# Weight conversions given steps of their own, relu and square over two banks, and a new order of products in a float32 convolution and two-layer feed-forward kernel

## The chip, the cores and the metric

The kernel runs on 1 core of a Trainium2 chip. The metric is the device time of one execution in microseconds (us). The trace is one profiled execution; its times count from the start of the span.

## What is computed

A causal convolution over 7 positions, with softmaxed taps per head, is followed by two feed-forward layers. Both multiply tokens of width 192 by a 192 x 2048 matrix, apply a gate, and multiply by a 2048 x 192 matrix. Everything is float32 and there are 8192 tokens.

```python
out[b, s, c] = sum_k softmax(weight)[head(c), k] * x_pad[b, s + k, c]
# first layer (n = 1)
h = x @ w_in
g = np.where(h >= 1, h, np.where(h <= -1, 0.0, (h + 1) ** 2 / 4))
x = g @ w_out
# second layer (n = 2)
h = x @ w_in
g = h * (1.0 / (1.0 + np.exp(-1.702 * h)))
out = g @ w_out
```

## The kernel before

**Tiles.** The tokens are cut into 16 blocks of T = 512. The matrices are cut into NF = 16 tiles of 128 hidden channels, two of which form a *group* (NG = 8 groups a layer). The 192 channels are 128 (part a) and 64 (part b). A *phase* is one layer on one block, 32 in all, and a *unit* is one phase with one hidden tile, 512 in all. The list `units` (L252) holds their order. Two neighbouring units are a *step*: step s is units 2s and 2s + 1.

**Precision.** Each float32 operand is split into a high part and a low part (`split`, L74: ACT casts the high part, DVE subtracts to get the low part), and a product is made of hi x hi, lo x hi and hi x lo.

**A step on TensorE.** `both(u, v)` (L379) makes the hidden products of units u, u + 1 (into PSUM banks h) and the output products of units v = u - 4 and v + 1, two steps back (into the accumulators acc). Every matmul uses 64 of the 128 rows, so one on the lower rows (`low`) and one on the upper rows (`up`) run side by side; `couples` (L346) issues the two lists in turn, 19 pairs a step. Where a bank changes from one half of the rows to the other, a pause waits for an earlier matmul (`at_signal`). There are four h banks, so a bank is written again two steps later.

**The gate.** Behind the products of a step, `act_a` and `act_b` (L281, L295) are recorded for each of its two units: in the first layer a relu (L288) and a square (L289) on ACT and a max/min (L290) on DVE, in the second layer one gelu (L292) on ACT; then a cast to ghi on ACT (L75) and a subtraction to glo on DVE (L76). ghi and glo feed the output products two steps later.

**Weights.** The float64 words of a group are fetched by 7 DMAs on the SP queue (`weight_load`, L103) into one of three `raw` buffers, and turned into float32 by five operations (`weight_ops`, L121): scale on ACT (L134), shift and join on DVE (L137, L140), the cast of the high part (L146), and the subtraction of the low part on DVE (L151, L156). The cast runs on ACT, but on DVE for groups 2 to 7 of the first layer (`BY_DVE`). Groups 0 and 1 are converted in the prologue, in two column parts each.

**The order.** Everything is recorded in program order, and each engine works through its own list. `convert_at` (L541) gives a group a first and a last unit; `at` and `beside` (L554) put the operations behind the gate of that step. Groups 6 and 7 of the first layer have their cast and subtraction behind the gate of step 9 and of step 11; their first products are in step 10 and step 12.

**The prologue.** Block 0 is convolved by DVE, block 1 by products with diagonal matrices on all 128 rows (`conv_on_pe`, L188, bank ca_ps). `first_only` (L369) makes the hidden products of steps 0 and 1 without output products; in step 0 they stand between the tap products of block 1. `put_a(1, ca_ps)` splits that block into xah and xal, which step 2 needs.

Of the kernel before, what the change touches and what calls it, by code (L numbers as in the profile page):

```python
# [15 lines left out]
P = 128  # L16
# [4 lines left out]
def kernel(  # L21
# [32 lines left out]
    IN = DB + 3 * P  # L54
    BY_DVE = {(1, g) for g in range(2, NG)}

# [5 lines left out]
    xs_p = ctx.enter_context(tc.tile_pool(name="xs", bufs=4))  # L62
    a_p = ctx.enter_context(tc.tile_pool(name="a", bufs=3))
    g_p = ctx.enter_context(tc.tile_pool(name="g", bufs=LAG))
# [56 lines left out]
    def weight_ops(n, g, s, tiles, cols=whole):  # L121
        low, high = s[:, cols, 0], s[:, cols, 1]
        w = wt[n][:, g]
        hi = w[:, DB + cols.start : DB + cols.stop]
        main = slice(max(cols.start, DB), min(cols.stop, WC - DB))

        def a():
            return tiles()[0][:, cols]

        def d():  # L130
            return tiles()[1][:, cols]

        def scale():
            nc.scalar.activation(a(), f32(high), AF.Prelu, scale=2.0**-112, alpha=-(2.0**32))  # L134

        def shift():
            nc.vector.tensor_single_scalar(d(), low, 29, op=ALU.logical_shift_right)  # L137

        def join():
            nc.vector.scalar_tensor_tensor(  # L140
                d(), a().bitcast(U32), 3, d(), op0=ALU.logical_shift_left, op1=ALU.bitwise_or
            )

        def high_part():
            cast = nc.vector.tensor_copy if (n, g) in BY_DVE else nc.scalar.copy
            cast(hi, f32(d()))  # L146

        def low_part():
            made = f32(tiles()[1])
            lo, hi = (slice(k + main.start, k + main.stop) for k in (WC + DB, DB))  # L150
            nc.vector.tensor_sub(w[:, lo], made[:, main], f32(w[:, hi]))  # L151
            if cols.stop == WC:
                ends = made.rearrange("p (n c) -> p n c", c=DB)[:, :: WC // DB - 1]
                wb = w[:, 0 : WC + 2 * DB].rearrange("p (n c) -> p n c", c=DB)
                lo, hi = (wb[:, k : WC // DB + 2 - k : WC // DB + 1 - 2 * k] for k in (0, 1))
                nc.vector.tensor_sub(lo, ends, f32(hi))  # L156
# [94 lines left out]

    units = in_turn((0, 4), (1, 4), *((0, 2), (1, 2), (0, 2)) * 3, (1, 6))  # L252
    units += in_turn((2, 8), (3, 8), (2, 8), (3, 8))
# [26 lines left out]

    def act_a(u):  # L281

        n, _ = phases[units[u][0]]
        h = hid.pop(u)
        a = a_p.tile([P, T], F32, tag="a", name="a")
        if n == 1:

            nc.scalar.activation(a, h, AF.Relu, bias=0.5, scale=0.5)  # L288
            nc.scalar.activation(a, a, AF.Square)  # L289
            nc.vector.scalar_tensor_tensor(a, h, 1.0, a, op0=ALU.max, op1=ALU.min)  # L290
        else:
            nc.scalar.activation(a, h, AF.Gelu_apprx_sigmoid)  # L292
        act[u] = a

    def act_b(u):  # L295
        a = act.pop(u)
        hi = g_p.tile([P, T], F32R, tag="ghi", name="ghi")
        lo = g_p.tile([P, T], F32R, tag="glo", name="glo")
        split(a, hi, lo)
        halves[u] = (hi, lo)  # L300

# [30 lines left out]
    def gemm2_pieces(us):  # L332
# [4 lines left out]
        def pieces(rows):  # L337
            a, b = [], []
            for wh, wl, wb, hi, lo in parts:
                a += [(acc_a, wl[rows], hi[rows]), (acc_a, wh[rows], hi[rows]), (acc_a, wh[rows], lo[rows])]  # L340
                b += [(acc_b, wb[rows], hi[rows]), (acc_b, wb[rows], lo[rows])]
            return a + b

        return pieces(slice(0, H)), pieces(slice(H, P))

# [17 lines left out]
    def hidden_banks(u):  # L363
        banks = {}
        for w in (u, u + 1):
            hid[w] = banks[HID + w % 4] = bank(HID + w % 4, f"h{w}")
        return banks

# [10 lines left out]
    def both(u, v):  # L379
# [6 lines left out]
        (low0, up0, b0), (low1, up1, b1) = gemm1_pieces(u), gemm1_pieces(u + 1)  # L386
        low, up = gemm2_pieces((v, v + 1))
        low = low0 + b0 + low1 + low
        up = up + up0 + up1 + b1
        p, f = units[v]  # L390
# [4 lines left out]
        fresh = {HID + u % 4, HID + (u + 1) % 4, *(acc_banks(p) if f == 0 else ())}  # L395
        couples(low, up, banks, fresh, closing, {3, 12, 20, 30})

# [51 lines left out]

    def weights_at(n, g):  # L450
        ops = []

        def piece():
            if (n, g) in raw:
                made = []
                ops.extend(weight_ops(n, g, raw.pop((n, g)), lambda: made or made.extend(weight_tiles()) or made))
            ops.pop(0)()

        return [piece] * 5

# [14 lines left out]
    with tc.manual_schedule():  # L475
# [49 lines left out]
        straight, crossed, last, closing = first_only(0)  # L525
        run(a1[0], straight, a1[1], crossed, a1[2], lambda: last(closing), *a1[3:])
        run(*w0[1], lambda: put_b(1, cb_ps), *w1_[1][0:3])
        act_a(0)
        act_a(1)
        run(*w1_[1][3:])  # L530
        act_b(0)
        act_b(1)
        straight, crossed, last, closing = first_only(2)
        run(straight, last, lambda: crossed(closing))
        put_a(1, ca_ps)
        act_a(2)
        act_a(3)
        act_b(2)
        act_b(3)

        def convert_at(n, g, begin, end):  # L541
            at(begin - 8, lambda: fetch_w(n, g))
            scale, shift, join, high, low = weights_at(n, g)
            for unit, op in zip((begin, begin, begin + 1, end, end), (scale, shift, join, high, low)):
                at(unit, op)

        for g in range(2, NG):
            convert_at(1, g, 4 * g - 8, 4 * g - 6)
        for g, (begin, end) in enumerate(((24, 26), (28, 30), (32, 32), (34, 34), (38, 40), (42, 42), (44, 44), (46, 46))):
            convert_at(2, g, begin, end)  # L550
        for j in range(1, NBLK // B):
            conv_at(j)

# [10 lines left out]
        for u in range(LAG, len(units) + LAG + 4, 2):  # L564
            v = u - LAG
# [8 lines left out]
            beside(u // 2)  # L574
            finish_if_last(v + 1, u + 1)
# [55 lines left out]
```

## Time and profile before

| | |
|---|---|
| runs before, median (lowest to highest) | 1151.12 us (1151.05 to 1152.19), 3 runs |
| the profiled execution's own time | 1151.66 us |
| its span | 1149.9 us |
| instructions in the trace | 23746 |
| busy: TensorE matmuls (PE), weight loads (PEld) | 98%, 80% |
| busy: ScalarE (ACT), VectorE (DVE) | 72%, 62% |
| mean granted TensorE clock | 0.996 of full speed |

The span starts and ends with work of the engines; the profiled time has 1.76 us more around it. PE busy counts a pipelined matmul from its start to its modelled end, so two matmuls side by side, or one waiting behind another, both count as busy; what a step costs is read from the starts of its matmuls.

### The profile page before, as it was taken

Reading aid. Unit: us, or ns where it says so; the run is one execution under the profiler, and the core shown is the slowest. Engines: PE = TensorE matmul, PEld = TensorE weight load, DVE = VectorE, ACT = ScalarE, POOL = GpSimd, SP = SyncE. Lnnn points to the kernel's source line nnn. Section 1 sums busy time; section 2 is a strip of 40 time slices with the busy share of each in tenths; the row PEclk is TensorE's granted clock in tenths of the full one; section 3 lists DMA queues with packets and bytes.
Section 4 is the critical chain, followed back from the end, with each engine's and each line's share of the span. In section 5 each row is a group of like instructions: output and inputs, shape, how many; then the busy total and the mean of one; then the engine's idle time right before and its main releaser. Section 6 shows DMA issues by size and latency. Waiting matters only on the chain.

```text
span 1149.9 us, 23746 instructions
## 1 busy us (share of the span) xinstructions
PE 1130.4 (98%) x9738; PEld 919.7 (80%) x9738; DVE 713.2 (62%) x1100; ACT 825.9 (72%) x1437; POOL 5.9 (1%) x12
## 2 busy tenths in 40 slices
PE   9979999999999999999999999999999999999998
PEld 5756778888888888888888888888888888888886
DVE  7957677675655756567565765657566575655532
ACT  7848758885867768586775867767686775867754
POOL 2000000000000000000000000000000000000000
PEclk9989999999999999999999999999999999999999
DMA  5413302000010000100001000010001000000000
GB/s 158 128 56 87 98 1 75 2 10 20 15 47 15 2 22 14 47 15 10 24 11 38 15 20 15 14 43 6 20 15 47 15 1 19 15 19 15 11 15 15
DMA packets 26476, 34.90 MB, mean 30 GB/s; under 512 B 3840, under 2 KB 16384, under 8 KB 26368
## 3 DMA queue, kind: packets, MB, share of 16 engines
q1 hardware_dynamic: 26224, 33.26, 10.4%
q8 instruction: 77, 1.26, 0.5%
q14 instruction: 31, 0.25, 0.1%
q10 hardware_dynamic: 144, 0.13, 0.0%
HBM read 18.96 MB, written 6.29 MB: 22 GB/s over the span
## 4 chain that ended last, share of the span: by engine, by line
PE 92%; DVE 3%; ACT 3%; issue 1%; SPq 1%; DMA 1%; DVEq 0%; ACTq 0%
PE acc L355 47%; PE h L355 43%; SPq L114 1%; ACT a L288 1%; DVE a L290 1%; ACT a L289 1%; DMA raw<-in_w_dram 1%; DVE wt L151 1%; ACT ghi L75 1%; PE cb_ps L195 1%; PE ca_ps L195 0%; DVE glo L76 0%; PE acc L329 0%; DVE wd L140 0%; ACT wa L134 0%
## 5 line engine op out<-in xcount | busy, mean ns | idle before, releaser
L355 PE MATMUL acc<-ghi,wt 64*128 64x512 f32 x3048 | 928.5, 388 | 0.2 <-ACT ghi L75 0.2
L355 PE MATMUL acc<-glo,wt 64*128 64x512 f32 x2032 | 750.8, 387 | 0.9 <-DVE glo L76 0.9
L355 PE MATMUL h<-xah,wt 64*128 64x512 f32 x2048 | 631.1, 389 | 12.5 <-DVE wt L146 9.3
L355 PEld LDWEIGHTS acc<-ghi,wt 64*128 64x128 f32 x3048 | 520.6, 185 | 60.5 <-ACT ghi L75 1.0
L76 DVE TENSOR_TENSOR glo<-a,ghi 128x512 fp32r<-128x512 f32 x512 | 341.2, 688 | 223.0 <-ACT ghi L75 211.5
L355 PEld LDWEIGHTS h<-xah,wt 64*128 64x128 f32 x2048 | 376.1, 185 | 60.3 <-DVE wt L146 10.6
L355 PEld LDWEIGHTS acc<-glo,wt 64*128 64x128 f32 x2032 | 375.2, 185 | 42.3 <-DVE glo L76 2.5
L355 PE MATMUL h<-xal,wt 64*128 64x512 f32 x1024 | 395.1, 387 | 0.7 <-DVE xal L76 0.7
L75 ACT CAST ghi<-a 128x512 fp32r<-128x512 f32 x512 | 301.9, 615 | 33.5 <-DVE a L290 33.2
L355 PE MATMUL h<-xbh,wt 64*128 64x512 f32 x1024 | 313.9, 388 | 0.0
L290 DVE SCALAR_TENSOR_TENSOR a<-h,a 128x512 f32<-128x512 f32 x256 | 176.4, 691 | 174.1 <-ACT a L289 173.7
L292 ACT ACTIVATE a<-h 128x512 f32<-128x512 f32 x256 | 150.6, 596 | 140.3 <-PE h L355 121.7
L355 PEld LDWEIGHTS h<-xal,wt 64*128 64x128 f32 x1024 | 188.4, 185 | 21.2 <-DVE xal L76 1.1
L355 PEld LDWEIGHTS h<-xbh,wt 64*128 64x128 f32 x1024 | 188.0, 185 | 21.0 <-ACT wt L146 0.8
L355 PE MATMUL h<-xbl,wt 64*128 64x512 f32 x512 | 197.5, 387 | 0.0
L288 ACT ACTIVATE a<-h 128x512 f32<-128x512 f32 x256 | 152.3, 595 | 61.3 <-PE h L355 52.8
L289 ACT ACTIVATE a<-a 128x512 f32<-128x512 f32 x256 | 161.8, 632 | 8.2
L355 PEld LDWEIGHTS h<-xbl,wt 64*128 64x128 f32 x512 | 94.1, 185 | 10.4 <-DVE xbl L76 0.2
L177 DVE SCALAR_TENSOR_TENSOR cva<-xt,taps,cva 128x512 f32<-128x512 f32 x90 | 67.5, 750 | 1.7
L75 ACT CAST xbh<-s 64x512 fp32r<-64x512 f32 x16 | 9.9, 620 | 38.7 <-DVE s L407 38.7
L177 DVE SCALAR_TENSOR_TENSOR cvb<-xt,taps,cvb 128x512 f32<-128x512 f32 x42 | 31.4, 748 | 0.7
L75 ACT CAST xah<-cva 128x512 fp32r<-128x512 f32 x15 | 9.3, 620 | 11.3 <-DVE cva L177 11.3
(62 smaller groups left out, 240.2 us busy)
## 6 DMA issues: line engine op xcount, KB each, us to landing
raw<-in_w_dram SPq DMA_DIRECT2D x48, 128.0 KB, 2.4
xt<-in_xa_dram SPq DMA_DIRECT2D x16, 259.0 KB, 2.8
xbh<-xbh SPq DMA_DIRECT2D x31, 128.0 KB, 2.2
xbl<-xbl SPq DMA_DIRECT2D x31, 128.0 KB, 2.2
out_dram<-o SPq DMA_DIRECT2D x15, 256.0 KB, 2.0
raw<-in_w_dram SPq DMA_DIRECT2D x48, 64.0 KB, 2.3
raw<-in_w_dram SPq DMA_DIRECT2D x16, 192.0 KB, 2.7
out_dram<-o SPq DMA_DIRECT2D x17, 128.0 KB, 2.3
```

Of the source, the lines that this page charges most:

```text
L75: nc.scalar.copy(hi, src)
L76: nc.vector.tensor_sub(lo, src, f32(hi))
L114: nc.sync.dma_start(s[rows, at : at + count], w[rows, c : c + count])
L151: nc.vector.tensor_sub(w[:, lo], made[:, main], f32(w[:, hi]))
L177: return lambda: nc.vector.scalar_tensor_tensor(c, x, w, c, op0=ALU.mult, op1=ALU.add)
L195: return lambda: nc.tensor.matmul(c, d[k], t[:, k : k + T], start=fresh and k == 0, stop=k == n - 1)
L288: nc.scalar.activation(a, h, AF.Relu, bias=0.5, scale=0.5)
L289: nc.scalar.activation(a, a, AF.Square)
L290: nc.vector.scalar_tensor_tensor(a, h, 1.0, a, op0=ALU.max, op1=ALU.min)
L292: nc.scalar.activation(a, h, AF.Gelu_apprx_sigmoid)
L355: mm = nc.tensor.matmul(banks[n], w, r, start=n in fresh, stop=ends.get(n) == k)
```

## The change

The cast of the high part runs on ACT for all groups. `convert_at` takes a step for the fetch and one for each of the five operations; the ACT operations (scale, high) stand inside the gate of their step, between square and ghi, and the DVE operations (shift, join, low) before the gate of theirs. `gates` replaces `act_a` and `act_b`: relu and square are single instructions over the two banks of a step (128 x 1024). The two h banks of a step are one tile. The products of a step stand in another order, with three signals for four. The units of the first two phases come in another order, in which groups 6 and 7 are first used in steps 11 and 12. In the prologue the hidden products of step 0 stand together, the fetches of groups 2 and 3 are recorded before the rest of the prologue's conversions, and `put_a(1, ca_ps)` after the gate of step 0.

```diff
-    BY_DVE = {(1, g) for g in range(2, NG)}
-    a_p = ctx.enter_context(tc.tile_pool(name="a", bufs=3))
+    a_p = ctx.enter_context(tc.tile_pool(name="a", bufs=2))
+    def pair_of_banks(u):
+        k = u // 2 % 2
+        return ps.tile([P, 2, T], F32, tag=f"pair{k}", name=f"pair{k}")
         def high_part():
-            cast = nc.vector.tensor_copy if (n, g) in BY_DVE else nc.scalar.copy
-            cast(hi, f32(d()))
+            nc.scalar.copy(hi, f32(d()))
-    units = in_turn((0, 4), (1, 4), *((0, 2), (1, 2), (0, 2)) * 3, (1, 6))
+    units = in_turn((0, 4), (1, 4), *((0, 2), (1, 2)) * 2, (0, 4), (1, 2), (0, 4), (1, 6))
-    def act_a(u):
+    def gates(u, conversions=()):
...
+        a = a_p.tile([P, 2, T], F32, tag="a", name="a")
         if n == 1:
             nc.scalar.activation(a, h, AF.Relu, bias=0.5, scale=0.5)
             nc.scalar.activation(a, a, AF.Square)
-            nc.vector.scalar_tensor_tensor(a, h, 1.0, a, op0=ALU.max, op1=ALU.min)
+            for op in conversions:
+                op()
+            for k in (0, 1):
+                nc.vector.scalar_tensor_tensor(a[:, k], h[:, k], 1.0, a[:, k], op0=ALU.max, op1=ALU.min)
         else:
-            nc.scalar.activation(a, h, AF.Gelu_apprx_sigmoid)
+            for k in (0, 1):
+                nc.scalar.activation(a[:, k], h[:, k], AF.Gelu_apprx_sigmoid)
+            for op in conversions:
+                op()
+        for k in (0, 1):
...
+            split(a[:, k], hi, lo)
+            halves[u + k] = (hi, lo)
-        low = low0 + b0 + low1 + low
-        up = up + up0 + up1 + b1
+        low = low1 + low_b + low0 + b0 + low_a
+        up = up0 + up_a + up1 + b1 + up_b
-        couples(low, up, banks, fresh, closing, {3, 12, 20, 30})
+        couples(low, up, banks, fresh, closing, {6, 18, 37})
+    def convert_at(n, g, fetch, scale, shift, join, high, low):
...
+        for k, (where, step) in enumerate(((act, scale), (dve, shift), (dve, join), (act, high), (dve, low))):
+            where.setdefault(step, []).append(lambda k=k: piece(k))
+        for op in ((1, 2, 0, 0, 1, 1, 1, 2), (1, 3, 0, 2, 2, 3, 3, 4), (1, 4, 1, 4, 4, 5, 5, 6), (1, 5, 2, 4, 5, 6, 6, 7)):
+            convert_at(*op)
+        for op in ((1, 6, 4, 7, 7, 8, 8, 9), (1, 7, 5, 8, 8, 9, 9, 10), (2, 0, 7, 10, 11, 11, 11, 12)):
+            convert_at(*op)
+        for op in ((2, 1, 8, 11, 12, 13, 13, 14), (2, 2, 11, 13, 14, 15, 15, 16), (2, 3, 12, 15, 16, 16, 16, 17)):
+            convert_at(*op)
+        for g in range(4, NG):
+            k = 10 + 2 * g
+            convert_at(2, g, k - 3, k - 1, k, k, k, k + 1)
-        run(a1[0], straight, a1[1], crossed, a1[2], lambda: last(closing), *a1[3:])
+        run(*a1[0:4], straight, last, lambda: crossed(closing), *a1[4:])
+        run(*of(fetches, 0))
+        gates(0, [*w1_[1][4:], *of(act, 0)])
...
+        run(*of(fetches, 1), lambda: put_a(1, ca_ps), *of(dve, 1))
+        gates(2, of(act, 1))
...
                 both(u, v)
-                for op in (act_a, act_b):
-                    op(u)
-                    op(u + 1)
+                run(*of(fetches, step), *of(dve, step))
+                gates(u, of(act, step))
```

**VectorE around group 6 of the first layer.** Its words lie in raw_528 before and in raw_486 after the change, their integer halves in wd_790 and wd_692; h18 and h19 are step 9, h20 and h21 step 10. Before:

```order
L290 SCALAR_TENSOR_TENSOR a_846<-h18_802,a_846 128x512
L290 SCALAR_TENSOR_TENSOR a_850<-h19_803,a_850 128x512
L76 TENSOR_TENSOR glo_855<-a_846,ghi_854 128x512
L76 TENSOR_TENSOR glo_859<-a_850,ghi_858 128x512
L146 CAST wt1_88<-wd_790 128x768
L151 TENSOR_TENSOR wt1_88<-wd_790,wt1_88 128x640
L156 TENSOR_TENSOR wt1_88<-wd_790,wt1_88 128x2x64
L290 SCALAR_TENSOR_TENSOR a_907<-h20_865,a_907 128x512
```

The cast and the subtraction stood behind all of step 9's gate, and step 10's first product reads them. Now (a_761 is the gate of step 8, a_820 that of step 9; the group's first product is in step 11):

```order
L143 SCALAR_TENSOR_TENSOR wd_692<-wa_691,wd_692 128x768
L140 TENSOR_SCALAR wd_759<-raw_558 128x768
L294 SCALAR_TENSOR_TENSOR a_761<-pair0_708,a_761 128x512 x2
L79 TENSOR_TENSOR glo_769<-a_761,ghi_768 128x512
L79 TENSOR_TENSOR glo_773<-a_761,ghi_772 128x512
L153 TENSOR_TENSOR wt1_88<-wd_692,wt1_88 128x640
L158 TENSOR_TENSOR wt1_88<-wd_692,wt1_88 128x2x64
L143 SCALAR_TENSOR_TENSOR wd_759<-wa_758,wd_759 128x768
L294 SCALAR_TENSOR_TENSOR a_820<-pair1_776,a_820 128x512 x2
```

The cast has left VectorE, and the subtraction stands ahead of step 9's gate, two steps ahead of the first product.

**ScalarE around the gate of step 0** (raw_105 is group 1, raw_222 group 2, ca_ps block 1). Before:

```order
L134 ACTIVATE wa_162<-raw_105 128x320
L288 ACTIVATE a_237<-h0_196 128x512
L289 ACTIVATE a_237<-a_237 128x512
L288 ACTIVATE a_241<-h1_197 128x512
L289 ACTIVATE a_241<-a_241 128x512
L146 CAST wt1_88<-wd_163 128x320
L75 CAST ghi_248<-a_237 128x512
L75 CAST ghi_252<-a_241 128x512
L75 CAST xah_137<-ca_ps_116 128x512
```

Now:

```order
L137 ACTIVATE wa_162<-raw_105 128x320
L148 CAST wt1_88<-wd_163 128x320
L289 ACTIVATE a_252<-pair0_196 128x1024
L290 ACTIVATE a_252<-a_252 128x1024
L137 ACTIVATE wa_257<-raw_222 128x768
L78 CAST ghi_262<-a_252 128x512
L78 CAST ghi_266<-a_252 128x512
L78 CAST xah_137<-ca_ps_116 128x512
```

The cast of group 1 now precedes the relu, and a scale of group 2 stands between square and ghi; xah_137, which step 2's first product reads, is still behind both ghi.

## Rows read from the trace of the kernel before

**Rows 1.** The page's first part: busy us (share of the span) and instructions of TensorE.

```profile
PE 1130.4 (98%) x9738; PEld 919.7 (80%) x9738; DVE 713.2 (62%) x1100; ACT 825.9 (72%) x1437; POOL 5.9 (1%) x12
```

**Rows 2.** TensorE's timeline, first products of four steps: start us, us, engine, line, operation.

```profile
21.97 0.39 PE L355 MATMUL h<-xah,wt 64*128 64x512 f32 x1
...
598.14 0.39 PE L355 MATMUL h<-xah,wt 64*128 64x512 f32 x1
...
611.06 0.39 PE L355 MATMUL h<-xah,wt 64*128 64x512 f32 x1
```

**Rows 3.** Relus and gelus from 0 to 598.2 us: count, ns, first and last start.

```profile
L288 ACT ACTIVATE a<-h x144: 577/598/606, 16.8 to 589.9; 128x512 f32<-128x512 f32 x144
L292 ACT ACTIVATE a<-h x115: 575/598/609, 106.9 to 597.2; 128x512 f32<-128x512 f32 x115
```

**Rows 4.** TensorE's timeline, 60 to 88 us; idle before and what ended it in brackets.

```profile
60.15 0.39 PE L355 MATMUL h<-xbl,wt 64*128 64x512 f32 x1
...
64.46 0.50 PE L355 MATMUL h<-xah,wt 64*128 64x512 f32 x1 [3.93 <-DVE wt L146]
...
71.14 0.39 PE L355 MATMUL h<-xah,wt 64*128 64x512 f32 x1
...
79.73 0.79 PE L355 MATMUL h<-xah,wt 64*128 64x512 f32 x1 [4.11 <-DVE wt L146]
...
87.29 0.39 PE L355 MATMUL h<-xah,wt 64*128 64x512 f32 x1
```

**Rows 5.** A window: length, busy us (count) of PE, PEld, DVE, ACT, POOL, granted clock, DMA.

```profile
80.00:90.00 10.00, 10.00 (x62) 7.77 (x64) 2.62 (x5) 3.44 (x6) 0.00 (x0) 0.70 0.05 17
```

**Rows 6.** VectorE's timeline: the cast of group 6.

```profile
63.86 0.55 DVE L146 CAST wt<-wd 128x768 fp32r<-128x768 f32 x1
```

**Rows 7.** Waits: who for whom, us in total, times, longest.

```profile
PE h L355 <- DVE wt L146: 9.3, 3, 4.1
```

**Rows 8.** TensorE's timeline around step 16, the first of the second layer.

```profile
99.98 0.39 PE L355 MATMUL h<-xbl,wt 64*128 64x512 f32 x1
...
101.15 0.49 PE L355 MATMUL h<-xah,wt 64*128 64x512 f32 x1 [0.78 <-ACT xah L75]
...
106.44 0.39 PE L355 MATMUL h<-xbl,wt 64*128 64x512 f32 x1
```

**Rows 9.** Groups of instructions by form: busy us, mean ns, idle before and its releasers.

```profile
L75 ACT CAST ghi<-a 128x512 fp32r<-128x512 f32 x512 | 301.9, 615 | 33.5 <-DVE a L290 33.2
L290 DVE SCALAR_TENSOR_TENSOR a<-h,a 128x512 f32<-128x512 f32 x256 | 176.4, 691 | 174.1 <-ACT a L289 173.7
L289 ACT ACTIVATE a<-a 128x512 f32<-128x512 f32 x256 | 161.8, 632 | 8.2
L288 ACT ACTIVATE a<-h 128x512 f32<-128x512 f32 x256 | 152.3, 595 | 61.3 <-PE h L355 52.8
L134 ACT ACTIVATE wa<-raw 128x768 f32<-128x768 f32 x14 | 12.8, 912 | 0.0
L146 ACT CAST wt<-wd 128x768 fp32r<-128x768 f32 x8 | 6.7, 834 | 8.4 <-DVE wd L140 8.4
L146 ACT CAST wt<-wd 128x448 fp32r<-128x448 f32 x2 | 1.1, 565 | 0.6 <-DVE wd L140 0.5
```

**Rows 10.** ScalarE's timeline in the prologue.

```profile
19.08 0.44 ACT L146 CAST wt<-wd 128x320 fp32r<-128x320 f32 x1
19.43 1.14 ACT L75 CAST ghi<-a 128x512 fp32r<-128x512 f32 x2
```

**Rows 11.** VectorE's timeline in the prologue: the last join of group 1.

```profile
17.40 0.49 DVE L140 SCALAR_TENSOR_TENSOR wd<-wa,wd 128x320 uint32<-128x320 uint32 x1
```

**Rows 12.** The SP queue's timeline: nine fetches, and a copy of block 1.

```profile
5.39 4.58 SPq L114 DMA_DIRECT2D raw<-in_w_dram  x9
16.19 0.50 SPq L207 DMA_DIRECT2D xbh<-xbh  x1
```

**Rows 13.** The page's part on DMA issues: KB each, us to landing.

```profile
raw<-in_w_dram SPq DMA_DIRECT2D x48, 128.0 KB, 2.4
xbh<-xbh SPq DMA_DIRECT2D x31, 128.0 KB, 2.2
```

More of the change, by code (lines that the diff above doesn't have):

```diff
@@ L279, in gemm1_pieces @@
         return *a, [(h, hi_b[r], bh[r]), (h, lo_b[r], bh[r]), (h, hi_b[r], bl[r])]
-    def act_a(u):
+    def gates(u, conversions=()):
         n, _ = phases[units[u][0]]
         h = hid.pop(u)
-        a = a_p.tile([P, T], F32, tag="a", name="a")
+        a = a_p.tile([P, 2, T], F32, tag="a", name="a")
         if n == 1:
@@ L289, in act_a @@
             nc.scalar.activation(a, a, AF.Square)
-            nc.vector.scalar_tensor_tensor(a, h, 1.0, a, op0=ALU.max, op1=ALU.min)
-        else:
-            nc.scalar.activation(a, h, AF.Gelu_apprx_sigmoid)
[L293 to L300, printed above, removed]
+            for op in conversions:
+                op()
+            for k in (0, 1):
+                nc.vector.scalar_tensor_tensor(a[:, k], h[:, k], 1.0, a[:, k], op0=ALU.max, op1=ALU.min)
+        else:
+            for k in (0, 1):
[3 more added lines that the diff above has]
+        for k in (0, 1):
+            hi = g_p.tile([P, T], F32R, tag="ghi", name="ghi")
+            lo = g_p.tile([P, T], F32R, tag="glo", name="glo")
+            split(a[:, k], hi, lo)
+            halves[u + k] = (hi, lo)
     def acc_banks(p):
@@ L341, in pieces @@
                 b += [(acc_b, wb[rows], hi[rows]), (acc_b, wb[rows], lo[rows])]
-            return a + b
-        return pieces(slice(0, H)), pieces(slice(H, P))
+            return a, b
+        return *pieces(slice(0, H)), *pieces(slice(H, P))
     def couples(low, up, banks, fresh, closing, at_signal):
@@ L363, in hidden_banks @@
     def hidden_banks(u):
[L364 to L367, printed above, removed]
+        h = hid[u] = pair_of_banks(u)
+        return {HID + (u + k) % 4: h[:, k] for k in (0, 1)}
     def first_only(u):
@@ L386, in both @@
         (low0, up0, b0), (low1, up1, b1) = gemm1_pieces(u), gemm1_pieces(u + 1)
-        low, up = gemm2_pieces((v, v + 1))
-        low = low0 + b0 + low1 + low
-        up = up + up0 + up1 + b1
+        low_a, low_b, up_a, up_b = gemm2_pieces((v, v + 1))
+        low = low1 + low_b + low0 + b0 + low_a
+        up = up0 + up_a + up1 + b1 + up_b
         p, f = units[v]
@@ L439 @@
     plan, xt, raw = {}, {}, {}
+    dve, act, fetches = {}, {}, {}
     def at(unit, op):
@@ L448, in fetch_w, with piece @@
             weight_load(n, g, s, cols)
[L450 to L459, printed above, removed]
+    def convert_at(n, g, fetch, scale, shift, join, high, low):
+        ops, made = [], []
+        def piece(k):
+            if not ops:
+                tiles = lambda: made or made.extend(weight_tiles()) or made
+                ops.extend(weight_ops(n, g, raw.pop((n, g)), tiles))
+            ops[k]()
+        fetches.setdefault(fetch, []).append(lambda: fetch_w(n, g))
+        for k, (where, step) in enumerate(((act, scale), (dve, shift), (dve, join), (act, high), (dve, low))):
+            where.setdefault(step, []).append(lambda k=k: piece(k))
     def fetch_x(*which):
@@ L518, in b0_low, with of @@
             nc.scalar.copy(b0l[DB:P], f32(b0l[0:DB]))
+        for op in ((1, 2, 0, 0, 1, 1, 1, 2), (1, 3, 0, 2, 2, 3, 3, 4), (1, 4, 1, 4, 4, 5, 5, 6), (1, 5, 2, 4, 5, 6, 6, 7)):
[7 more added lines that the diff above has]
+            convert_at(2, g, k - 3, k - 1, k, k, k, k + 1)
+        for j in range(1, NBLK // B):
+            conv_at(j)
+        def of(ops, step):
+            return ops.get(step, [])
         w0, w1_ = parts_of(0), parts_of(1)
@@ L525 @@
         straight, crossed, last, closing = first_only(0)
-        run(a1[0], straight, a1[1], crossed, a1[2], lambda: last(closing), *a1[3:])
[L527 to L532, printed above, removed]
+        run(*a1[0:4], straight, last, lambda: crossed(closing), *a1[4:])
+        run(*of(fetches, 0))
+        run(*w0[1], lambda: put_b(1, cb_ps), *w1_[1][0:4])
+        gates(0, [*w1_[1][4:], *of(act, 0)])
         straight, crossed, last, closing = first_only(2)
         run(straight, last, lambda: crossed(closing))
[L535 to L552, printed above, removed]
+        run(*of(fetches, 1), lambda: put_a(1, ca_ps), *of(dve, 1))
+        gates(2, of(act, 1))
         def beside(step):
@@ L564 @@
         for u in range(LAG, len(units) + LAG + 4, 2):
-            v = u - LAG
+            v, step = u - LAG, u // 2
             if u < len(units):
                 both(u, v)
-                for op in (act_a, act_b):
-                    op(u)
-                    op(u + 1)
+                run(*of(fetches, step), *of(dve, step))
+                gates(u, of(act, step))
             elif v < len(units):
@@ L573 @@
                 gemm2(v + 1)
-            beside(u // 2)
+            beside(step)
             finish_if_last(v + 1, u + 1)
```

## The prediction

> **What bounds the kernel now.** I read the page first: TensorE's matmuls are busy 98% of the span [rows 1]. Busy counts overlapping matmuls, so I went to TensorE's own timeline and measured steps. In the middle of the run a step starts every 4.307 us: three steps lie between 598.14 and 611.06 [rows 2]. That is 0.227 us for each of its 19 pairs, evenly spaced, so nothing is lost there and the change removes no product. By 598.2 us, 259 relus and gelus have started, two a step [rows 3]; the last is the first of step 129, so the start at 598.14 is that of step 130. From step 2 at 21.97 [rows 2] that is 128 steps in 576.17 us. At 4.307 they would take 551.3. **24.9 us are lost, all in the early part; that is what there is to win.**
>
> The timeline of that part shows where. Step 9 ends at 60.15 + 0.23 = 60.38, but step 10 starts at 64.46, released by VectorE's cast of weights; step 13 starts at 87.29 [rows 4]. Steps 10, 11 and 12 thus take 26.91 us for 12.92: 14.0 lost. Two waits of 3.9 and 4.1 us are 8.0 of it; some 4 us more come from the clock, which the window behind the second wait shows at 0.70, a mixture of the 2.4 and 1.2 GHz levels [rows 5]; the rest is the subtraction behind the cast. The cast ran at 63.86 [rows 6], after step 10 should have begun, because it stood behind the whole gate of step 9, which needs step 9's products. Three waits on this cast make 9.3 us [rows 7]. Another place is step 16, the first of the second layer: its last pair starts 6.46 us after that of step 15 [rows 8], so 2.15 us are lost on the first layer's output being split. The other 8.8 us lie in smaller waits, mostly on weights and on ACT.
>
> **The change, part by part.**
>
> *Conversions in steps of their own.* Each group's last operation now stands ahead of a gate one to three steps before its first product, so by the order TensorE no longer meets it. This returns the 14.0 us of steps 10 to 12, clock included, and the waits on weights elsewhere. I count the whole 24.9 as returned, and now charge what comes in its place.
>
> *Step 2 starts later.* Step 2's first product needs xah of block 1, cast by ACT behind the gate of step 0. ACT's cast of group 1, which ran at 19.08 [rows 10], now precedes the relu and must wait for a join that ended at 17.40 + 0.49 = 17.89 [rows 11]. From there: cast 0.44, relu 1.03, square 1.06, scale 0.91, two ghi in 1.14 and xah 0.6 [rows 9, 10] end at 23.07, less up to 0.4 for overlap (two ghi take 1.14 where two durations are 1.23). That is 0.7 to 1.1 us later than 21.97, and xal behind it on DVE may add 0.3. I take **1.0**, bounds 0.7 to 1.4. Putting step 0's products together saves TensorE some switches between 128-row and 64-row work, but I cost it at nothing: step 2 waits for ACT all the same. On SP, 14 fetches of 4.58/9 = 0.51 us each [rows 12] now stand ahead of block 1's two copies. Only the second seven can be held, for group 0's buffer; if they began no earlier than the copy did before, at 16.19, the copies would go out at 19.8 and 20.3 and land 2.2 us later [rows 13], by 22.5. Their first use is pair 10 of step 2, after 25, so they stay hidden; a delay beyond 2.5 us would stall TensorE. POOL's list is not changed.
>
> *Relu and square over 1024 columns.* No row has this width. ACT's casts go from 565 ns at 448 columns to 834 at 768 [rows 9], 0.84 ns a column; 512 more columns make 595 into 1.03 us and 632 into 1.06. The lower bound is no growth (0.6), the upper one two whole instructions (1.19 and 1.26). By the slope, 128 first-layer steps save ACT 0.36 us each. In the steady state that is worth nothing, as TensorE is evenly fed already.
>
> *Does the gate still fit a step?* relu 1.03, square 1.06, a max/min on DVE 0.69, two ghi 1.24 [rows 9]: 4.02, with four handovers of some 0.04 about 4.2 us against 4.31. Now both h banks close at pair 14 of 19, where they closed at 12 and at 18. From that matmul's end, 3.6 us into the step, relu, square and two max/min end at 7.1, and the banks are due at 8.61: 1.5 us to spare. So plain steps cost **0**.
>
> *Gates with conversions.* In steps 2 to 15 ACT also runs nine scales (0.91) and eight casts (0.83); six casts have come from VectorE, where one took 0.55 [rows 6, 9]. One of them fits into ACT's wait for the max/min. Five steps (4, 8, 11, 13, 15) have two: 1.03 + 1.06 + 1.74 + 1.24 = 5.07, less five overlaps of 0.09, is 4.6 to 4.7, some 0.4 over a step. If the 1.5 us did not absorb any of it, five times 0.4 is **2.0**; bounds 0 and 3.
>
> *Step 16.* The same chain remains (copy, add, casts, a DMA of 2.2 us), behind a wider gate, and b1's products move from pairs 16 to 18 to pairs 12 to 14, 0.9 us sooner. The nearest row is its own loss of 2.15 [rows 8]; I take **2.3**, bounds 1.0 and 3.5.
>
> *Steps 17 to 28.* Second-layer weights now lead by at least one step. What stays is ACT and DVE sharing conversions with the next blocks' convolution: **1.0**, bounds 0 and 2.5.
>
> *The new order of products and signals.* The same 19 pairs. Every bank's change of halves still lies four pairs (0.9 us) behind the signalled matmul, and pauses at three pairs cost nothing before: **0**. A fetch lands 2.4 us after its issue [rows 13]; group 2's goes out right behind the prologue's fetches, and every later one stands two or three steps, 8.6 us or more, ahead of its scale: 0.
>
> *Sum.* 24.9 - 1.0 - 2.0 - 2.3 - 1.0 = 18.6 us. The profiled execution took 1151.66, which makes 1133.1; the median of the runs, 1151.12, lies 0.54 below it, so **1132.5**. With all low bounds 1.7 us are lost again (1127.9), with all high ones 10.4 (1136.6).
>
> **The rivals.**
>
> *ScalarE becomes the bound of steps 2 to 15.* Scale and cast stand between square and ghi, and ACT takes its list in order. If they fill no wait, a step costs 4.02 + (9 x 0.91 + 8 x 0.83)/14 = 5.1 us, 0.8 over, for 14 steps 11.4 instead of 2.0: 1141.9. For it: six casts are 0.28 us dearer here than on VectorE. Against it: the max/min takes 0.69, in which ACT is free, so one conversion a step costs nothing. Chance 0.11. The Trainium skill, "ScalarE: Activation LUTs", Rules for kernel authors, says the opposite of what the change does: cheap elementwise work such as relu, max and add belongs on VectorE. By that rule this rival would be the case; the rows support the price, 0.83 against 0.55 us for one cast, but not that VectorE had the room.
>
> *Slower: the wide instructions do not scale.* If a read over two banks costs well above two reads, the plain gate no longer fits. A step's 4.2 us may grow by 0.1. At 1.4 us each (0.36 above my price) the gate takes 4.9, 0.6 over; eight steps of a phase fall 4.8 behind, less 1.5 of slack 3.3, in 15 phases some 50 us: about 1182. It loses to before from about 1.25 us each. Against it: the slope over three widths, and two separate instructions would be 1.19 and 1.26 at most. Chance 0.04.
>
> *The waits on weights only move.* If a buffer or a late fetch makes one group late again, one such wait with its clock costs half of 14.0: 1139.5; both leave 1146.5. Against it: the fetch distances above. Chance 0.05.
>
> **How the numbers follow.** The forecast has 0.80. Its bounds reach from 1127.9 to 1136.6; going on towards the first and third rival to 1140 leaves out under 0.2: range 1128 to 1140. A measurement of this kernel can tell about 0.2%, 2.3 us. Faster by more: the forecast, the first rival and nearly all of the third, 0.93. Within 0.2%: 0.03, from mild cases of the second and bad ones of the third. Slower: 0.04.
>
> **What would show it.** Right: no matmul wait on weights above 1 us, a clock of 1.00 in all windows from 20 to 160 us, step 13 starting near 70 us, relu at 1.03 and square at 1.06, steps of 4.31 from 200 us on. Step 2 should start near 23, and step 16 should still show a wait on xah. The first rival would show steps of 5 us from 25 to 80 with PE waiting for ghi or h banks; the second, relu above 1.2 us and steps above 4.31 at 600 us. The forecast is wrong if the steady step changes at all, since some 240 of them follow the early part.

## The result and the profile after

The changed kernel takes 1133.56 us (median of five executions; 1133.43 to 1133.98), the kernel before 1151.69 us (median of six; 1151.05 to 1152.95). The ratio is 0.9842, 95% interval 0.9829 to 0.9856: 18.1 us, or 1.6%, faster. Forecast: 1132.5. (A sixth execution of the changed kernel took 2308.9 us, for a reason that no run here shows, and is left out.) The profile after is that of run 1 below, with a span of 1131.8 us.

TensorE has the same 9738 matmuls as in [rows 1] in a shorter span, and the relu and square are now 128 instructions each where [rows 9] had 256. From the page after:

```profile
PE 1122.0 (99%) x9738; PEld 934.4 (83%) x9738; DVE 698.0 (62%) x1094; ACT 781.8 (69%) x1187; POOL 5.9 (1%) x12
...
L289 ACT ACTIVATE a<-pair 128x1024 f32<-128x1024 f32 x128 | 131.2, 1025 | 32.4 <-PE pair L359 17.5
L290 ACT ACTIVATE a<-a 128x1024 f32<-128x1024 f32 x128 | 135.9, 1062 | 4.1
```

TensorE's timeline after shows where its time went. A step's first products are the `pair<-xah` row with x4. The rows are step 2, step 3, steps 12 and 13, steps 15, 16 (with a late pair inside it) and 17, steps 44 to 46, and step 130:

```profile
23.38 0.73 PE L359 MATMUL pair<-xah,wt 64*128 64x512 f32 x4 [1.01 <-ACT xah L78]
...
28.22 0.62 PE L359 MATMUL pair<-xah,wt 64*128 64x512 f32 x4
...
66.98 0.62 PE L359 MATMUL pair<-xah,wt 64*128 64x512 f32 x4
...
71.28 0.62 PE L359 MATMUL pair<-xah,wt 64*128 64x512 f32 x4
...
79.92 0.62 PE L359 MATMUL pair<-xah,wt 64*128 64x512 f32 x4
...
85.65 0.73 PE L359 MATMUL pair<-xah,wt 64*128 64x512 f32 x4 [1.24 <-ACT xah L78]
...
90.28 0.49 PE L359 MATMUL pair<-xbh,wt 64*128 64x512 f32 x1 [1.12 <-DMA xbh<-xbh]
...
91.76 0.84 PE L359 MATMUL pair<-xah,wt 64*128 64x512 f32 x4
...
208.44 0.64 PE L359 MATMUL pair<-xah,wt 64*128 64x512 f32 x4
...
214.09 0.73 PE L359 MATMUL pair<-xah,wt 64*128 64x512 f32 x4 [1.15 <-ACT ghi L78]
...
218.55 0.62 PE L359 MATMUL pair<-xah,wt 64*128 64x512 f32 x4
...
580.31 0.62 PE L359 MATMUL pair<-xah,wt 64*128 64x512 f32 x4
```

The four bracketed rows are all the waits that the view shows for TensorE from step 2 to 250 us. Both long waits of [rows 4] on a cast of weights are gone, and no wait on weights is left. From step 2 to step 130 it takes 580.31 - 23.38 = 556.93 us, against 551.3 for 128 steps at 4.307: **5.6 us lost where 24.9 were.** Step 2 starts 23.38 - 21.97 = 1.41 later, so 24.9 - 5.6 - 1.4 = 17.9 of the 18.1 us lie here. The window that stood at a granted clock of 0.70 [rows 5] now reads:

```profile
80.00:90.00 10.00, 7.91 (x65) 5.55 (x61) 9.01 (x15) 8.87 (x13) 0.00 (x0) 1.00 0.12 28
```

### The profile page after: what moved, and what is told of

It reads as the page before. It is cut to its first block, busy times and chain, and to the rows that moved or that the text cites. A ratio compares the mean times of both kernels' runs of the same rounds, so it can differ in the third digit from the quotient of the medians.

```text
span 2306.8 us, 23878 instructions
## 1 busy us (share of the span) xinstructions
PE 2301.7 (100%) x9738; PEld 1448.2 (63%) x9738; DVE 699.7 (30%) x1094; ACT 791.3 (34%) x1187; POOL 5.9 (0%) x12
## 4 chain that ended last, share of the span: by engine, by line
PE 100%; ACT 0%; DMA 0%; DVE 0%; issue 0%; ACTq 0%
PE acc L359 51%; PE pair L359 47%; PE cb_ps L197 1%; PE ca_ps L197 0%; PE acc L333 0%; DMA taps<-in_taps_dram 0%; ACT diag L194 0%; ACT o L436 0%; ACT taps L91 0%; DVE taps L95 0%; DVE taps L90 0%; DVE sm L93 0%; DVE mx L89 0%; DVE sm L92 0%; DVE sm L94 0%
## 5 line engine op out<-in xcount | busy, mean ns | idle before, releaser
L359 PE MATMUL acc<-ghi,wt 64*128 64x512 f32 x3048 | 1291.0, 671 | 0.0
L359 PE MATMUL acc<-glo,wt 64*128 64x512 f32 x2032 | 1038.8, 671 | 0.0
L359 PEld LDWEIGHTS acc<-ghi,wt 64*128 64x128 f32 x3048 | 749.7, 295 | 260.8 <-issue 235.7
L359 PE MATMUL pair<-xah,wt 64*128 64x512 f32 x2048 | 820.3, 671 | 0.2
L359 PEld LDWEIGHTS pair<-xah,wt 64*128 64x128 f32 x2048 | 452.7, 296 | 179.2 <-issue 134.7
L359 PE MATMUL pair<-xbh,wt 64*128 64x512 f32 x1024 | 529.0, 671 | 0.0
L359 PE MATMUL pair<-xal,wt 64*128 64x512 f32 x1024 | 514.5, 671 | 0.0
L359 PEld LDWEIGHTS pair<-xbh,wt 64*128 64x128 f32 x1024 | 301.0, 295 | 87.1 <-issue 80.6
L359 PE MATMUL pair<-xbl,wt 64*128 64x512 f32 x512 | 342.6, 672 | 0.0
L289 ACT ACTIVATE a<-pair 128x1024 f32<-128x1024 f32 x128 | 131.1, 1024 | 605.4 <-PE pair L359 585.0
L359 PEld LDWEIGHTS pair<-xal,wt 64*128 64x128 f32 x1024 | 226.6, 296 | 86.7 <-issue 80.4
```

What stands on the lines that cost most here:

```text
L359: mm = nc.tensor.matmul(banks[n], w, r, start=n in fresh, stop=ends.get(n) == k)
```

## Experiments

Each ran beside the kernel before on its chip; medians of it there were 1152.0 to 1152.3 us. The runs are on three chips, and a ratio's interval reaches some 1.7 us to either side, so a difference of 1 or 2 us between two of them is a hint and no more, unless their traces show where it comes from.

**1. The changed kernel once more.** No edit.

> The changed kernel once more, for its profile and time. The prediction: 1132.5 us; step 2 starts near 23, step 13 near 70 us, the granted clock stays at 1.00, step 16 waits for xah, and a step takes 4.31 us at 600 us. The rival of a bound ScalarE: 1142, with steps of about 5 us between 25 and 80 us.

Measured 1133.77 us, ratio 0.9842 (0.9825 to 0.9858). The rows above are from it, and the runs below are measured against it.

**2. Only the place of conversions, in the kernel before.** Everything else stays as before, the casts on DVE too.

```diff
-            convert_at(1, g, 4 * g - 8, 4 * g - 6)
+            convert_at(1, g, 4 * g - 10, 4 * g - 8)
```

> The kernel before, with one edit: the conversions of groups 2 to 7 of the first layer begin and end one step earlier, in the same engines and the same old order. If the 14.0 us of steps 10 to 12 came from the place of the conversions alone, waits and clock together, the two long waits shrink to under 2 us, the clock stays up, and the time falls by 9 to 13 us, to 1139 to 1143. If they came from ScalarE and VectorE being overloaded there, moving the work by a step only moves the waits, and the time stays within 3 us of 1151.

Measured 1140.36 us, ratio 0.9898 (0.9883 to 0.9913): 11.7 us from one step's shift. TensorE's waits on weights between 60 and 75 us shrink from 3.93 and 4.11 [rows 4] to these two, and the clock of that window is whole:

```profile
61.84 0.50 PE L355 MATMUL h<-xah,wt 64*128 64x512 f32 x1 [0.36 <-DVE wt L151]
...
71.07 0.50 PE L355 MATMUL h<-xah,wt 64*128 64x512 f32 x1 [0.28 <-DVE wt L151]
```

```profile
60.00:70.00 10.00, 9.64 (x83) 7.49 (x82) 8.86 (x15) 8.58 (x15) 0.00 (x0) 1.00 0.44 121
```

The shift has a price of its own, so 11.7 is what is left of more: the first product of step 4 now waits 1.30 us for a max/min on VectorE, and the clock falls in two windows, 30 to 40 and 90 to 100 us, that stood at 1.00 in the kernel before.

```profile
32.70 0.50 PE L355 MATMUL h<-xah,wt 64*128 64x512 f32 x1 [1.30 <-DVE a L290]
```

```profile
30.00:40.00 10.00, 8.55 (x59) 6.34 (x57) 9.58 (x17) 8.47 (x16) 0.00 (x0) 0.83 0.67 194
...
90.00:100.00 10.00, 9.42 (x68) 8.18 (x70) 7.21 (x12) 7.72 (x13) 0.00 (x0) 0.83 0.40 106
```

So the place of first-layer conversions makes two thirds of the gain, without the wide instructions, the new order of products or the casts on ACT. How the other third is shared out is only in part known: the new place of the second layer's conversions was not tried by itself.

**3. The reverse: only two subtractions put back, in the changed kernel.** The last subtractions of groups 6 and 7 go behind the gate of the step before their use; `tail` is a new table whose operations run behind `gates`.

```diff
-        ... ((act, scale), (dve, shift), (dve, join), (act, high), (dve, low))
+        ... ((act, scale), (dve, shift), (dve, join), (act, high), (tail if n == 1 and g > 5 else dve, low))
-        (1, 6, 4, 7, 7, 8, 8, 9), (1, 7, 5, 8, 8, 9, 9, 10)
+        (1, 6, 4, 7, 7, 8, 8, 10), (1, 7, 5, 8, 8, 9, 9, 11)
                 gates(u, of(act, step))
+                run(*of(tail, step))
```

> The changed kernel with only two operations moved: the last subtractions (VectorE, some 0.9 us each) of first-layer groups 6 and 7 stand behind the gate of the step before their first product (steps 10 and 11, products at steps 11 and 12), the place that conversions had in the kernel before. By my theory a gate's last subtraction ends some 4 us into the next step, so TensorE waits about 4 to 5 us at step 11 and as long at step 12, two waits as in the kernel before, and the granted clock falls behind them, which costs some 4 us more: 1145 to 1149. Rival A (the clock does not follow from such waits): the waits alone, 1142 to 1144, with a clock of 1.00 in 60 to 90 us. Rival B (an operation's place counts little, the number of operations on VectorE and ScalarE beside the gates is what matters): within 2 us of 1133.7.

Measured 1147.73 us, ratio 0.9960 (0.9946 to 0.9973): 14.0 us slower than the changed kernel. TensorE's timeline shows steps 11 (from 62.61), 12 (from 73.19) and 13, and the windows of it the granted clock, the column behind the engines:

```profile
62.61 0.39 PE L359 MATMUL pair<-xah,wt 64*128 64x512 f32 x2
67.62 0.80 PE L359 MATMUL pair<-xah,wt 64*128 64x512 f32 x2 [4.62 <-DVE wt L153]
...
73.19 0.39 PE L359 MATMUL pair<-xah,wt 64*128 64x512 f32 x2
78.75 0.79 PE L359 MATMUL pair<-xah,wt 64*128 64x512 f32 x2 [5.16 <-DVE wt L153]
...
85.51 0.62 PE L359 MATMUL pair<-xah,wt 64*128 64x512 f32 x4
```

```profile
67.00:70.00 3.00, 2.38 (x12) 1.91 (x14) 2.19 (x4) 0.00 (x0) 0.00 (x0) 0.52 0.20 52
70.00:73.00 3.00, 3.00 (x28) 2.45 (x26) 0.00 (x0) 0.51 (x1) 0.00 (x0) 0.91 0.62 168
...
81.00:84.00 3.00, 3.00 (x16) 2.30 (x14) 0.00 (x0) 0.00 (x0) 0.00 (x0) 0.50 0.03 5
84.00:87.00 3.00, 3.00 (x28) 2.50 (x26) 0.06 (x1) 2.09 (x2) 0.00 (x0) 0.96 0.00 0
```

Two steps take 85.51 - 62.61 = 22.90 us for 8.61, so 14.3 are lost, nearly what steps 10 to 12 lost before (14.0). The waits are 4.62 + 5.16 = 9.8 of it. Of the other 4.5 us, 4.2 come behind the waits: 18 pairs stand between 67.62 and 73.19, and 18 between 78.75 and 85.51, which take 5.57 and 6.76 us where 18 at 0.227 take 4.08. There the clock reads 0.50 to 0.52 at first, the 1.2 GHz level, and 16 matmuls start in 3 us where 28 do at 0.96. Both rivals fall: the clock follows these waits (A), and no operation was added (B). The Trainium skill, "TensorE: Matmul & The Clock Gate" (HAM oscillation — how this bites in real kernels), describes such a chain, with waits for DMA: TensorE waits for data, and the work behind the wait starts at half clock. The rows at 0.50 agree.

**4. Relu and square as one instruction per bank**, the rest as changed.

```diff
-            nc.scalar.activation(a, h, AF.Relu, bias=0.5, scale=0.5)
-            nc.scalar.activation(a, a, AF.Square)
+            for k in (0, 1):
+                nc.scalar.activation(a[:, k], h[:, k], AF.Relu, bias=0.5, scale=0.5)
+                nc.scalar.activation(a[:, k], a[:, k], AF.Square)
```

> The changed kernel, with relu and square again as one instruction for each bank (four of 512 columns for two of 1024). The prediction's reason (the wide form saves ScalarE 0.36 us a step, but TensorE is not waiting for it): at most 2 us slower than the changed kernel, no more than a few waits of under 0.5 us between 55 and 100 us. The rival (ScalarE is the bound of steps 2 to 15, and the wide form is what makes the gates fit): 14 steps of 0.36, 5 us slower or more.

Measured 1134.8 us (1134.03 to 1135.41), ratio 0.9851 (0.9837 to 0.9866): 1.0 us slower by the medians, while its profiled execution has the span of run 1's (1131.9 against 1131.8). The wide instructions as such are worth little, if anything.

**5. The old order of products and signals**, the rest as changed.

```diff
-        low = low1 + low_b + low0 + b0 + low_a
-        up = up0 + up_a + up1 + b1 + up_b
+        low = low0 + b0 + low1 + low_a + low_b
+        up = up_a + up_b + up0 + up1 + b1
-        couples(low, up, banks, fresh, closing, {6, 18, 37})
+        couples(low, up, banks, fresh, closing, {3, 12, 20, 30})
```

> The changed kernel, with the products of a step in the order of the kernel before and its four signals. The prediction costed the new order at nothing in itself; but with gates over both banks the old order closes the second bank at pair 18 instead of 14, so relu starts 0.9 us later, and the first output products are due at pair 0 instead of 3. By the spare time of 1.5 us a plain step still fits and the steady step stays at 4.31 us; waits of up to 0.5 us appear in steps with conversions and splits, 1 to 12 us in all. If the order of products mattered to the pace of the pairs itself, the steady step would change at 600 us: by 0.05 us for 240 steps, 12 us, either way.

Measured 1146.92 us, ratio 0.9958 (0.9943 to 0.9973): 13.1 us slower, a little past the range I had given. The plain step is 4.31 us long, and yet every first-layer phase lost time. ScalarE's timeline of one phase, and the wait it causes on TensorE:

```profile
548.88 1.03 ACT L289 ACTIVATE a<-pair 128x1024 f32<-128x1024 f32 x1 [2.19 <-PE pair L359]
...
553.19 1.03 ACT L289 ACTIVATE a<-pair 128x1024 f32<-128x1024 f32 x1 [0.21 <-PE pair L359]
...
557.31 0.59 ACT L426 COPY o<-acc 64x512 f32<-64x512 f32 x1
557.92 0.59 ACT L429 COPY o<-acc 128x512 f32<-128x512 f32 x1
558.40 1.03 ACT L289 ACTIVATE a<-pair 128x1024 f32<-128x1024 f32 x1
...
584.13 1.09 ACT L297 ACTIVATE a<-pair 128x512 f32<-128x512 f32 x2 [0.21 <-PE pair L359]
```

```profile
562.00 0.47 PE L359 MATMUL pair<-xah,wt 64*128 64x512 f32 x1 [0.23 <-ACT ghi L78]
```

Relus start 4.31 apart, until two copies of the finished phase's output stand in front of one: it starts 5.21 behind its predecessor. The eight steps take 584.13 - 548.88 = 35.25 us; in the changed kernel and in second-layer phases they take 34.45. So 0.8 is lost once in each of the 12 first-layer phases behind 236 us, some 9 us; the rest is lost before that. The same two copies stand in front of a relu in the changed kernel too. There it starts 5.27 behind its predecessor, and the phase still takes 34.46 us (first relu 540.87, first gelu of the next phase 575.33):

```profile
545.15 1.03 ACT L289 ACTIVATE a<-pair 128x1024 f32<-128x1024 f32 x1
...
550.42 1.03 ACT L289 ACTIVATE a<-pair 128x1024 f32<-128x1024 f32 x1
```

In the old order the second bank closes with pair 18, in the new one both are closed by pair 14; those four pairs, 0.9 us, are room that the copies need. The old order also has its first output products, which read ghi, at pair 0 instead of 3, so ghi is due 0.7 us sooner; no run changes that alone.

**6. The old order and, besides, one instruction per bank** (the edits of 5 and 4 together).

> The changed kernel with the old order of products and signals (as the run that took 1146.9) and, besides, relu and square as one instruction per bank, so that the first relu can start when the first h bank closes, at pair 12, and not with the second at pair 18. If the 13 us that the old order costs come from the wide relu having to wait for both banks: a first-layer phase is back at 34.45 us for 8 steps and the time is 1134 to 1140. If they come from the order itself (the banks' changes of halves, the signals, the late close of the second bank): a phase stays near 35.2 and the time at 1145 to 1148.

Measured 1138.79 us, ratio 0.9888 (0.9871 to 0.9904). A first-layer phase takes 34.55 us, so 8.1 of the 13.1 us return, though the output products still come at pair 0. Most of the cost thus comes from a wide relu that has to wait for the later of two banks. With 4 and 5 this gives a table (us):

| | wide relu and square | one per bank |
|---|---|---|
| new order | 1133.8 | 1134.8 |
| old order | 1146.9 | 1138.8 |

The new order is worth 4.0 us with separate instructions and 13.1 with wide ones; the wide ones lose 8.1 in the old order, and what they gain in the new one, 1.0, is too little to tell. Neither price exists by itself.

**7. The six casts back on VectorE**, at the same place in the list.

```diff
-            nc.scalar.copy(hi, f32(d()))
+            (nc.vector.tensor_copy if (n, g) in {(1, k) for k in range(2, NG)} else nc.scalar.copy)(hi, f32(d()))
```

> The changed kernel, with the six casts of first-layer groups 2 to 7 given back to VectorE (0.55 us each there, 0.83 on ScalarE), in the same place: between the gate's squares and its max/min. My theory: in the changed kernel ScalarE is 9.0 to 9.8 us busy in each 10 us from 20 to 80 us, and yet steps 3 to 15 take 4.31, so relieving it gains nothing; on VectorE the casts stand ahead of the gate's max/min, which frees the h banks. Time 1133 to 1136. Rival (ScalarE as the bound, by which such work belongs on VectorE): it gains some of the 3 us that the early part still loses, 1130 to 1132.5.

Measured 1134.75 us (1134.62 to 1134.92), ratio 0.9848 (0.9834 to 0.9863): 1.0 us slower by the medians, and certainly no gain. ScalarE is freer, but VectorE is at 9.70 of 10 us where it was at 9.10, and new waits on ghi appear at steps 8 and 11 (the window is 50 to 60 us, columns as in [rows 5]):

```profile
50.00:60.00 10.00, 10.00 (x90) 8.49 (x90) 9.70 (x17) 9.49 (x13) 0.00 (x0) 1.00 0.37 102
```

```profile
49.76 0.73 PE L359 MATMUL pair<-xah,wt 64*128 64x512 f32 x4 [0.25 <-ACT ghi L78]
...
63.29 0.72 PE L359 MATMUL pair<-xah,wt 64*128 64x512 f32 x4 [0.30 <-ACT ghi L78]
```

**8. The old order of units** in the first two phases.

```diff
-    units = in_turn((0, 4), (1, 4), *((0, 2), (1, 2)) * 2, (0, 4), (1, 2), (0, 4), (1, 6))
+    units = in_turn((0, 4), (1, 4), *((0, 2), (1, 2), (0, 2)) * 3, (1, 6))
```

> The changed kernel with the old order of units in steps 4 to 15 (groups 4 and 6 of block 0's first layer are used one step earlier, at steps 7 and 10). If the place of the conversions gives nearly all of the gain and the order of units is only an adjustment to it: each of the two groups then has its last subtraction one step before its use, or in the same step's front, and TensorE waits up to about 1 us at step 7 and step 10: 1134 to 1136. If the order of units is an equal part of the gain, long waits of 3 us or more with a lower granted clock return at step 7 or 10: 1140 or more.

Measured 1135.45 us, ratio 0.9856 (0.9841 to 0.9871): 1.7 us slower, with waits on the last subtraction of 0.62 at step 7 and 0.88 at step 10. The order of units only gives the place its last bit of room.

**9. Block 0's first layer ended one step sooner.**

```diff
-    units = in_turn((0, 4), (1, 4), *((0, 2), (1, 2)) * 2, (0, 4), (1, 2), (0, 4), (1, 6))
+    units = in_turn((0, 4), (1, 4), *((0, 2), (1, 2)) * 2, (0, 8), (1, 8))
```

> The changed kernel with block 0's first layer ended one step sooner (steps 10 and 11 are its groups 6 and 7, steps 12 to 15 are block 1's). Step 16, which waits for block 0's first-layer output, has a step (4.31 us) more for that chain, so its waits of 1.24 on xah and 1.12 on the copy of xbh should go: up to 2.5 us less, 1131 to 1132.5, if nothing takes their place. Rival: group 6 is now used at step 10, one step after its subtraction on VectorE, and TensorE waits there, or the finish of phase 0 delays the gate of its own step: as much is lost again, 1133 to 1135.

Measured 1134.58 us, ratio 0.9847 (0.9832 to 0.9861): the rival holds. The waits on xah and xbh at step 16 are gone, and two others stand in their place, one on weights at step 10, and one on ghi, whose gate now stands behind ScalarE's copy and two casts of block 0's output (81.08 to 83.11; the relu behind them starts at 83.02, 6.63 us after the one before):

```profile
59.66 0.50 PE L359 MATMUL pair<-xah,wt 64*128 64x512 f32 x2 [0.90 <-DVE wt L153]
...
86.60 0.73 PE L359 MATMUL pair<-xah,wt 64*128 64x512 f32 x4 [0.82 <-ACT ghi L78]
```

**10. The start of step 2 as before**: the cast of group 1 behind the relu and square, the scale of group 2 behind xah.

```diff
-        run(*w0[1], lambda: put_b(1, cb_ps), *w1_[1][0:4])
-        gates(0, [*w1_[1][4:], *of(act, 0)])
+        run(*w0[1], lambda: put_b(1, cb_ps), *w1_[1][0:3])
+        gates(0, w1_[1][3:])
-        run(*of(fetches, 1), lambda: put_a(1, ca_ps), *of(dve, 1))
+        run(lambda: put_a(1, ca_ps), *of(fetches, 1), *of(act, 0), *of(dve, 1))
```

> The changed kernel with three things in the first two steps as in the kernel before: ScalarE's cast of group 1's second half behind the relu and square of step 0 (it stood ahead of them and waited for VectorE's join), the scale of group 2 behind the cast of block 1's xah, and that cast's code ahead of the fetches. If the later start of step 2 (23.38 us against 21.97) comes from the cast ahead of the relu and the scale ahead of xah, step 2 starts 0.5 to 1.4 us sooner, near 22 to 22.9, and the whole time is as much shorter, 1132.3 to 1133.3, since nothing behind it has a wait of its own to give back. If it comes from the order of step 0's products (the relu has to wait for the pair of banks), step 2 stays within 0.3 us of 23.38 and the time at 1133.5 to 1134.

Measured 1133.51 us (1133.13 to 1136.3), ratio 0.9833 (0.9820 to 0.9846): no difference from 1133.77 that can be told. The profiled execution is the one of 1136.3; all its rows from 14 us on are 2.1 us later than in run 1, so only distances can be read. ScalarE's timeline:

```profile
19.97 1.02 ACT L289 ACTIVATE a<-pair 128x1024 f32<-128x1024 f32 x1 [0.87 <-PE pair L359]
...
23.91 1.16 ACT L78 CAST ghi<-a 128x512 fp32r<-128x512 f32 x2 [1.47 <-DVE a L294]
```

And VectorE's:

```profile
22.47 0.43 DVE L153 TENSOR_TENSOR wt<-wd,wt 128x256 fp32r<-128x256 f32 x1 [2.15 <-ACT wt L148]
22.81 0.28 DVE L158 TENSOR_TENSOR wt<-wd,wt 128x128 fp32r<-128x128 f32 x1
23.12 1.29 DVE L294 SCALAR_TENSOR_TENSOR a<-pair,a 128x512 f32<-128x512 f32 x2
```

Less 2.1, the relu starts at 17.9 instead of 18.75, but ghi starts at 21.8 and not sooner than in run 1 (21.63). The 0.9 us won ahead of the relu is lost in the wait for the max/min. VectorE's rows show why: the subtraction of group 1 stands ahead of the max/min, waits 2.15 us for the cast that was moved back, and ends when the max/min starts. Step 2 starts at 25.60, less 2.1 at 23.5, and the time is 1133.51, as the second theory had them, and the relu does wait for its pair of banks (0.87). But the cast ahead of the relu costs 0.9 there, as the first theory had it; it only isn't to be won by this move. Neither describes the whole.

No version beat the changed kernel by more than a measurement can tell.

## Why the prediction was right

The result lies 1.1 us above the forecast, inside the range. Point by point:

- **What there is to win, and why.** "24.9 us lost, all in the early part" and "14.0 of it in steps 10 to 12, clock included" hold: run 2 removes the two waits in the kernel before and gains 11.7, run 3 makes two such waits in the changed kernel and loses 14.3 in two steps, 4.2 of them by the clock ("some 4 us").
- **Gates with conversions: 2.0 charged, 0 measured.** Steps 3 to 14 take 79.92 - 28.22 = 51.70 us; twelve steps of 4.307 are 51.68. ScalarE's timeline of a step with a cast and a scale shows why:

```profile
66.57 1.02 ACT L289 ACTIVATE a<-pair 128x1024 f32<-128x1024 f32 x1
...
71.47 1.02 ACT L289 ACTIVATE a<-pair 128x1024 f32<-128x1024 f32 x1
...
75.59 1.02 ACT L289 ACTIVATE a<-pair 128x1024 f32<-128x1024 f32 x1
```

  The two relus are 4.90 apart, 0.59 more than a step, the next two 4.12: the 1.5 us to spare took all of it. My low bound was the right one.
- **Step 2: 1.0 charged, 1.9 measured.** It starts 1.41 later, and lasts 28.22 - 23.38 = 4.84, which is 0.53 too long. That is beyond my bound of 1.4. The chain was the one I named. It was 0.35 late from its start, as the join began at 17.75 and not at 17.40, and the xal that I said "may add 0.3" was left out of the 1.0: the pair that reads it starts at 24.23, 0.85 behind the step's first where 0.45 is the pace.
- **Step 16: 2.3 charged, 3.2 measured.** It starts 1.42 later than 4.31 behind step 15 and lasts 91.76 - 85.65 = 6.11, 1.80 too long. The wait on xah was forecast. The 1.12 on the copy of xbh was not: I took 2.2 us for this DMA, and it landed 3.9 behind its issue at 86.38. The view of the tile xbh around step 16, in run 1 and then in run 7, and the pair that reads the copy first in run 7, without a wait:

```profile
DMA to landing us min/median/max: 3.9/3.9/3.9
...
DMA to landing us min/median/max: 2.2/2.2/2.2
...
90.03 0.39 PE L359 MATMUL pair<-xbh,wt 64*128 64x512 f32 x1
```

  A copy of 2.2 would have landed at 88.6, ahead of 88.77, where the pair was due. The b1 products that come "0.9 us sooner" only make the wait longer. In runs 1, 3, 4, 8 and 10 the copy took 3.5 to 4.1 us, and TensorE waited 0.8 to 1.4 for it; in the kernel before and in runs 2, 5, 6, 7 and 9 it took 2.2, and TensorE did not wait. What lengthens it no run shows.
- **Steps 17 to 28: 1.0 charged, 0.4 measured**, from 17 to 44: 208.44 - 91.76 = 116.68 for 27 x 4.307 = 116.28.
- **A wait I had not placed: 1.5 at step 45.** Step 44 takes 5.65 and step 45 takes 4.46. From block 2 on, block 2's is the only first-layer phase followed by another first-layer phase, so its output is split beside full gates: the cast of xbh (209.98 to 210.60) stands in front of a relu, which starts 6.03 us behind its predecessor (210.51 against 204.48). It is in part a price of the wide form: in run 4, with one instruction per bank, steps 44 and 45 take 218.64 - 209.44 = 9.20 us and lose 0.6.
- **The new order of products: 0 charged, 0 to see**, and still the weakest step of the text. I priced the wide gate by the banks closing at pair 14, and the order by its pauses, as if they were two edits. Run 5 shows one of them without the other at 13.1 us. It changed no term of the sum; what I missed is that the order was the condition of the wide gate.
- **Wide instructions:** 1025 and 1062 ns against 1.03 and 1.06 from the slope.
- **The marks named:** no wait on weights, a clock of 1.00 in all windows from 20 to 160 us, steps of 4.31 from 218 us on (I had said 200; steps 44 and 45 lie between), a wait on xah at step 16. Step 2 was to start near 23 and step 13 near 70; they start at 23.38 and 71.28.

The sum: 1.9 + 0 + 3.2 + 0.4 + 1.5 = 7.0 lost again instead of 6.3; the 24.9 less 7.0 is 17.9. That 6.3 and 7.0 lie so close is partly luck: 2.6 us too much for the gates and for steps 17 to 28 stand against 3.3 too little at steps 2, 16 and 45.

The first rival fell (its price is 10.8 by its own terms, 5.08 less 4.307 for 14 steps, and not 11.4; nothing rests on that): ScalarE is 9.0 to 9.8 us busy in each 10 us from 20 to 80 us, and TensorE does not wait for it in steps 3 to 15. The rule of the Trainium skill's "ScalarE: Activation LUTs" (Rules for kernel authors), cheap elementwise work such as relu, max and add belongs on VectorE, would have the six casts back there if it is read to cover casts; run 7 did that and gained nothing (1134.75 against 1133.77). The cast is cheaper on VectorE, but the max/min behind it is what ScalarE's ghi waits for (82.3 us in all, by the view of waits). The second rival fell with the two durations, the third with the absence of any wait on weights.

## What to carry to other kernels

An operation that prepares data for step s must not stand, on its engine, behind work that needs the products of step s - 1, however little it takes itself: here two subtractions of 1.0 us each in the wrong place cost 14 us, some 4 of them by the clock that fell behind the waits. Before pricing a wider instruction, ask when the last of its inputs is complete: here it cost 8.1 us without an order that completes them early enough for the work that sometimes stands in front. And an engine that is 98% busy in a window, as ScalarE was from 50 to 60 us, need not be the bound: the slack of 1.5 us behind it took up what one crowded step added.

## What was not expected

In run 5 a loss of 0.8 us once per first-layer phase, in a place where every plain step has its full pace, cost some 9 us; it can be seen in phase lengths, not in the step. And behind the late copy of xbh (90.28 us), which held up one half of the rows, the two halves of the pairs no longer start together: the weight loads then read busy for all of a window (10.00 of 10 us from 100 to 110), but the next steps start 4.31 apart, so this share says nothing of the pace. That the late copy is the cause is not shown: in run 8, with such a wait too, the share is 8.35 in that window.

```profile
100.00:110.00 10.00, 10.00 (x92) 10.00 (x90) 7.86 (x13) 7.43 (x14) 0.00 (x0) 1.00 0.68 196
```
